# Loading the last 4 KB per partition of wq apart, in transfers of 120 and of 8 partitions

## The chip, the cores and the metric

The kernel runs on one core of a Trainium2 chip. The core has five engines, each with its own instruction queue: PE (TensorE, matrix products), DVE (VectorE), ACT (ScalarE), POOL (GpSimd) and SP (SyncE). Here SP issues nearly all transfers. The transfers themselves run on 16 DMA engines that work beside the five. The metric is the device time of one execution in microseconds (us), as the median over several runs.

## What is computed

One decoding step of a small network for two sequences (B = 2) with one new token each, D = 512. A block of grouped-query attention over a cache of 32,768 positions (32 query heads, 8 key and value heads, head size 128) is joined with a small gated MLP. Cut to what matters:

```python
xn = layernorm(x)
q = (xn @ wq).reshape(B, 1, 32, 128)                   # wq: 512 x 4096
scores = einsum("bhqd,bhkd->bhqk", q, repeat(k_cache, 4)) * 128 ** -0.5
o = einsum("bhqk,bhkd->bhqd", softmax(scores), repeat(v_cache, 4))
s = o.reshape(B, 1, 4096) @ wo                         # wo: 4096 x 512
h2 = gelu(layernorm(x1) @ w3) @ w4                     # the MLP
g = silu(x1 + h2)
return x + s * g
```

With one token per sequence the shifted terms of the mixer are zero, so x1 equals xn, and w1 and w2 aren't needed. All data are bf16. The two caches hold 2 x 8 x 32,768 x 128 x 2 bytes = 134 MB each. They, wq (4 MB), w3, w4 and wo are each read once.

## The kernel before, in words

The work goes over 16 groups, one for each pair of sequence and key head. A group's keys are one transfer of 128 partitions with 64 KB each into `kbuf`, its values one such transfer into `vbuf`. Only the last group is cut into halves. For each group DVE transposes the keys in blocks (line 589), PE forms the scores (line 698), ACT takes the exponentials (line 491), and PE multiplies with the values (line 722). When ACT has seen the end of a group's value products (line 495), SP may issue the next load of values (line 448). When PE has passed the first half of the scores, SP may issue the next load of keys (line 464).

Before the groups there is a prologue. SP issues, in this order and without any wait, wq (line 310, into the third slot of `kbuf`), w3 and w4 (lines 311 and 312, into `vbuf`), the keys of group 0 (line 313), and two small loads of x (line 330). ACT issues one small load of x (line 318). DVE normalises x, and PE transposes it. DVE's copy of the result to `xT` (line 395) is the instruction that waits for wq, with `(d_wq, 16)`. Then PE forms q (line 403), and the MLP's products follow (lines 424 and 439). The load of group 0's values (line 448) waits for the last MLP product, since it overwrites w3 and w4. Four small transfers (line 457) put the gate `g` into the layout of the output.

After the groups comes wo, in six transfers (`wo_parts`, lines 477 and 479). SP issues all of them when ACT has seen the end of the next to last use of their place. PE multiplies each part as it arrives (lines 760 and 768), DVE forms the gated sum (lines 647 and 648), and SP and ACT each store half of the output (line 651).

SP issues in program order. A transfer moves one stretch of memory for each partition row, and the profile counts such stretches as packets. Its semaphore has gone up by 16 when all of it has landed.

`wo_parts` reuses the semaphores of the prologue's loads for its six parts: the first part counts on `d_wq`. `n_wo` holds the value that each part's users wait for.

Of the kernel before, what the change touches and what calls it, by code (L numbers as in the profile page):

```python
# [118 lines left out]
def kernel(  # L119
# [16 lines left out]
    B, Sq, D = A_x.shape  # L136
    _, Hkv, Sk, Dh = A_k_cache.shape
    HD = A_wq.shape[1]
# [4 lines left out]
    DK = D // 128  # L143
# [10 lines left out]
    NQ = 4  # L154
# [3 lines left out]
    OQ = 2  # L158
# [80 lines left out]
    NG = len(groups)  # L239
    wo_parts = [(0, 4, 0, NQ), (4, 5, 0, NQ), (5, 6, 0, NQ), (6, 7, 0, NQ), (7, 8, 1, NQ), (7, 8, 0, 1)]  # L240

    KW = wo_parts[0][1]
    RW = KW * NQ
    FILL = (1, 1)
# [22 lines left out]
    sp = Queue(nc.sync, None)  # L267
# [5 lines left out]
    d_wq, d_w3, d_w4, d_x, d_x4, d_g = (sem(f"d_{n}") for n in ("wq", "w3", "w4", "x", "x4", "g"))  # L273
    d_wo = [d_wq, d_w3, d_w4, d_x, d_x4, d_g]
    assert len(d_wo) == len(wo_parts)
    n_wo = [16, 16, 16, 16, 16 * OQ, 16 * NQ]
    for i in range(len(wo_parts)):
        n_wo[i] += 16

# [7 lines left out]
    kbuf_wq = kbuf[:, 2 * SLOT:3 * SLOT]  # L287
# [19 lines left out]
    with tc.tile_critical(sync_engine=mybir.EngineType.Pool, no_gpsimd_drain=True):  # L307
        nc.scalar.wait_ge(t_shift, n_out).then_inc(t_shift, -n_out)

        sp.op(lambda e: e.dma_start(out=kbuf_wq[:, 0:DK * HD], in_=A_wq.rearrange("(p k) f -> p (k f)", k=DK)), inc=(d_wq, 16))  # L310
        sp.op(lambda e: e.dma_start(out=vbuf[:, 0:W4O], in_=B_w3.rearrange("(p k) f -> p (k f)", k=DK)), inc=(d_w3, 16))
        sp.op(lambda e: e.dma_start(out=vbuf[:, W4O:W4O + FK * D], in_=B_w4.rearrange("(p f) d -> p (f d)", f=FK)), inc=(d_w4, 16))
        sp.op(lambda e: e.dma_start(out=kbuf[:, 0:NPART * SLOT], in_=row_view(A_k_cache, *groups[0])), inc=(t_k[0], 16))
# [9 lines left out]
            out=ident[:, :], in_=ident[:, :], compare_op=ALU.not_equal, fill=1.0, base=0,  # L323
# [14 lines left out]
        e = ve.op(lambda e: e.tensor_copy(out=xf[:, :], in_=x_bf[:, :]), (d_x, 16))  # L338
# [14 lines left out]
        e = e_xn = layernorm(xn, xf, "ln1", e)  # L353
        ve.op(lambda v: v.tensor_copy(out=xs_bf[0:B, :], in_=xn[:, :]), e_xn, e_xs0)
        e = layernorm(ln2, xn, "ln2", e_xn)
        e_xs = ve.op(lambda v: v.tensor_copy(out=xs_bf[32:32 + B, :], in_=ln2[:, :]), e, e_id)  # L356
        with nc.allow_low_precision(reason="one of the terms is one, the others are zero"):
            e = ve.op(lambda v: v.tensor_reduce(
                out=sel0[:, :], in_=ident[:, :].rearrange("p (n w e) -> p w n e", n=NB, e=2), axis=AX.XY, op=ALU.add), e_id)
            e_quad = ve.op(lambda v: v.tensor_reduce(  # L360
                out=quad[:, :], in_=ident[:, :].rearrange("p (j w) -> p j w", j=4), axis=AX.X, op=ALU.add))
        ve.op(lambda v: v.tensor_reduce(
            out=cls[:, :, :], in_=ident[:, :].rearrange("p (n w e) -> p n e w", n=NB, e=2), axis=AX.X, op=ALU.add))
        e_sel = ve.op(lambda v: v.tensor_copy(out=sel[:, :, :], in_=sel0[:, :].unsqueeze(1).broadcast_to([128, 4, 32])), e)
        ve.op(lambda v: v.tensor_reduce(
            out=sel_o[:, :, :],
            in_=ident[:, :].rearrange("p (j a t h) -> p a t h j", j=4, t=VT, h=rep)[:, 0, :, :, :],
            axis=AX.X, op=ALU.add))
        e_selh = ve.op(lambda v: v.tensor_reduce(
            out=sel_h[:, :], in_=ident[:, :].rearrange("p (r h) -> p h r", h=rep), axis=AX.X, op=ALU.add))  # L370
        e_row = ve.op(lambda v: v.tensor_reduce(
            out=row_of[:, :], in_=ident[:, :].rearrange("p (r h) -> p r h", h=rep), axis=AX.X, op=ALU.add))
# [3 lines left out]
            out=comb[:, OJ - 1::OJ], in_=ident[:, :].rearrange("p (n c) -> p c n", n=NQ)[:, 0:B, :], axis=AX.X, op=ALU.add), e_c0)  # L376
        ve.op(lambda v: v.tensor_reduce(
            out=mask[:, :], in_=ident[:, :].rearrange("p (h w) -> p h w", h=rep), axis=AX.X, op=ALU.add))
        ve.op(lambda v: v.tensor_scalar_mul(
            out=same_h[:, :].rearrange("p (r h) -> p r h", h=rep),  # L380
            in0=sel_h[:, :].unsqueeze(1).broadcast_to([128, 32, rep]), scalar1=-inv_sqrt_dh), e_selh)
        e_const = ve.op(lambda v: v.tensor_copy(
            out=sel_w[:, :, :], in_=row_of[:, :].unsqueeze(1).broadcast_to([128, 4, 32])), e_row, e_ones)
# [7 lines left out]
        treg = qrb[:, :].bitcast(BF16)  # L391
        for k in range(DK):
            e = pe.op(lambda t, k=k: t.transpose(  # L393
                out=treg[:, 64 * k:64 * k + 32 + B], in_=xs_bf[:, k::DK], identity=ident[0:32 + B, 0:32 + B]), e_xs)
        e_xT = ve.op(lambda v: v.tensor_copy(
            out=xT[:, :, :].rearrange("p (s k) b -> p s k b", s=2),
            in_=treg[:, 0:64 * DK].rearrange("p (k s c) -> p s k c", k=DK, s=2)[:, :, :, 0:B]), e, (d_wq, 16))
        HH = Hq // NPART
        for i in range(NPART):
            for k in range(DK):  # L400
                for n in range(NQ):
                    last = k == DK - 1 and n == NQ - 1
                    e = pe.op(lambda t, i=i, k=k, n=n: t.matmul(
                        sc[i][32 * n:32 * n + B, :], lhsT=xT[:, k, :],
                        rhs=wq3[:, k, :].rearrange("p (h n y) -> p h n y", n=NQ, y=32)[:, i * HH:(i + 1) * HH, n, :],
                        start=(k == 0), stop=(k == DK - 1), tile_position=(0, 32 * n)),
                        e_xT, e_s00, inc=last)
            e = ve.op(lambda v, i=i: v.transpose(out=qT[:, i * 512:(i + 1) * 512], in_=sc[i][:, :]), e)
        e_q = ve.op(lambda v: v.tensor_mul(
            out=q_sb[:, :, :, :].rearrange("p n e (b h) -> p (n e) b h", b=B),  # L410
            in0=qT[:, :].rearrange("p (h c) -> p c h", c=32)[:, 0:B, :].unsqueeze(1).broadcast_to([128, 2 * NB, B, Hq]),
            in1=cls[:, :, :].rearrange("p n e -> p (n e)").unsqueeze(2).unsqueeze(3).broadcast_to([128, 2 * NB, B, Hq])), e)
        e = pe.op(lambda t: t.matmul(
            qrb[:, 0:NB * 2 * B * Hq], lhsT=sel[:, :, :].rearrange("p j w -> p (j w)"),
            rhs=q_sb[:, :, :, :].rearrange("p n e c -> p (n e c)"), start=True, stop=True), e_q, e_sel)
        e_qr = ve.op(lambda v: v.tensor_copy(
            out=qr[:, :, :, :, :].rearrange("p n e b h -> p (n e b h)"), in_=qrb[:, 0:NB * 2 * B * Hq]), e)
# [3 lines left out]
        for k in range(DK):  # L421
            for n in range(NQ):
                last = k == DK - 1 and n == NQ - 1
                e = pe.op(lambda t, k=k, n=n: t.matmul(
                    pro[32 * n:32 * n + B, 0:FQ], lhsT=xT[:, DK + k, :],
                    rhs=w3v[:, k, n * FQ:(n + 1) * FQ].rearrange("p (y f) -> p f y", y=32),
                    start=(k == 0), stop=(k == DK - 1), tile_position=(0, 32 * n)), (d_w3, 16), inc=last)
        e = ve.op(lambda v: v.transpose(out=h4[:, :], in_=pro[:, 0:FQ]), e)
        e_hf = ve.op(lambda v: v.tensor_copy(
            out=hf[:, :].rearrange("p (f b) -> p f b", b=B), in_=h4[:, :].rearrange("p (f c) -> p f c", c=32)[:, :, 0:B]), e)  # L430
        e = ve.op(lambda v: v.tensor_mul(out=x2[:, :], in0=hf[:, :], in1=hf[:, :]), e_hf)
        e = ve.op(lambda v: v.tensor_scalar(out=x2[:, :], in0=x2[:, :], scalar1=0.044715, scalar2=1.0, op0=ALU.mult, op1=ALU.add), e)
        e = ve.op(lambda v: v.tensor_mul(out=inner[:, :], in0=hf[:, :], in1=x2[:, :]), e)
        e = ac.op(lambda v: v.activation(out=th[:, :], in_=inner[:, :], func=ACT.Tanh, scale=GELU_C), e)
        e = ve.op(lambda v: v.tensor_scalar(out=th[:, :], in0=th[:, :], scalar1=0.5, scalar2=0.5, op0=ALU.mult, op1=ALU.add), e)
        e = ve.op(lambda v: v.tensor_mul(out=h_bf[:, :], in0=hf[:, :], in1=th[:, :]), e, (d_w4, 16))
# [6 lines left out]
        e = ac.op(lambda v: v.activation(out=sig[:, :], in_=t_f[:, :], func=ACT.Sigmoid), e_tf)  # L443
# [17 lines left out]
        for m in range(1, NG):  # L461
            base = m % 2
            if m < NG - 1:
                sp.op(lambda e, m=m, base=base: e.dma_start(
                    out=kbuf[:, base * SLOT:(base + NPART) * SLOT], in_=row_view(A_k_cache, *groups[m])),
                    (pe.sem, pe_0 + m), e_q, inc=(t_k[0], 16))
            else:
                for i, h in enumerate(order(m)):
                    sp.op(lambda e, m=m, h=h, base=base: e.dma_start(
                        out=kbuf[:, (base + h) * SLOT:(base + h + 1) * SLOT],  # L470
                        in_=row_view(A_k_cache, *groups[m])[:, h * SLOT:(h + 1) * SLOT]),
# [14 lines left out]
        with nc.Fori(0, NG // 2, engines=[ACTE]):  # L486
            for par in range(2):
                take(nc.scalar, t_shift)
                for h in range(NPART):
                    i = order(par).index(h)  # L490
                    nc.scalar.activation(  # L491
                        out=ep[i][:, :], in_=sc[i][:, :], func=ACT.Exp, scale=inv_sqrt_dh, bias=shift[:, :],
# [84 lines left out]
        with nc.body("dve_groups", valid_engines=[DVE]):  # L577
            c = Counts()
            for par in range(2):
                nc.vector.wait_ge(*c(t_z))  # L580
                for i, h in enumerate(order(par)):
                    u = par + h
                    kt = kbuf[:, u * SLOT:(u + 1) * SLOT].bitcast(I32)
                    for r in range(NR):
                        n = i * NR + r
                        events = ([c(t_k[i], 16)] if r == 0 else []) + ([used(par, n - T_BUFS)] if n >= T_BUFS else [])
                        for e in events[:-1]:
                            nc.vector.wait_ge(*e)
                        ins = nc.vector.transpose(  # L589
                            out=Ts[n % T_BUFS][:, :].rearrange("p (b t k) -> p t b k", b=NB, t=RT),  # L590
                            in_=kt[:, r * W:(r + 1) * W].rearrange("p (t b k) -> p t b k", b=NB, t=RT))
# [10 lines left out]
                for h in range(NPART):  # L602
                    e = c(t_e)
# [33 lines left out]
        c = Counts()  # L637
# [174 lines left out]
```

## Time and profile before

| what | value |
|---|---|
| median of 3 runs | 655.92 us (655.91 to 655.99) |
| profiled execution, span from first to last instruction | 654.1 us |
| PE busy in the span | 417.4 us (64%) |
| DVE busy | 379.4 us (58%) |
| ACT busy, POOL busy | 39.7 us, 10.3 us |
| bytes moved | 280.54 MB, mean 429 GB/s |
| share of 16 DMA engines on SP's queue (q1) | 99.2% |

The profiled execution gives its span and no total of its own. The span and the median differ by 1.8 us, which lies before the first and behind the last instruction or in the profiling.

The profile has a page with busy times, slices, queues, the chain that ended last and groups of instructions. Its trace can be asked for a window of time. A view of DMA for a window gives two rows of 40 equal slices (the busy share of the 16 engines in tenths, where 9 means 90% or more, and GB/s). Below stand the packets that started in the window and, per queue, packets, MB, and the time of these packets as a share of 16 engines over the window. So share x 16 x window / packets is the mean time of a packet, and a share can go over 100% where packets run out of the window. A row of the timeline gives start, duration, engine, line, operation, operands and count. In brackets stands how long the engine was idle before and who ended that. "SPq" is an issue by SP, not the transfer.

### The profile page before, as it was taken

How to read it: one execution, taken by the hardware profiler on the slowest of the kernel's cores; microseconds unless marked ns; L12 is line 12 of the kernel's file. 1: busy time of each engine (PE TensorE's matmuls, PEld its weight loads, DVE VectorE, ACT ScalarE, POOL GpSimd, SP SyncE). 2: the span in 40 equal slices, each digit the busy share in tenths (PEclk: the TensorE clock that was granted, in tenths of full speed). 3: DMA queues.
4: the chain of work that ended last, by engine and by line, in shares of the span. 5: the costliest groups of instructions: out<-in, count | busy, mean ns of one | idle time of the engine just before them, and what ended most of it. 6: DMA issues, size and time to landing. Idle time of an engine off the chain costs nothing. (4 is left out here: it accounts for less than half of the span.)

```text
span 654.1 us, 6304 instructions
## 1 busy us (share of the span) xinstructions
PE 417.4 (64%) x2476; PEld 159.3 (24%) x2476; DVE 379.4 (58%) x541; ACT 39.7 (6%) x90; POOL 10.3 (2%) x44
## 2 busy tenths in 40 slices
PE   1437386574858747485774838667484865748876
PEld 0013132221313212131321313222131322213223
DVE  5348193673919457291854729276481936738772
ACT  1200101000010100001000010100001010000101
POOL 1000000000000000000000000000000000000000
PEclk9859889697997969899796989969698896979999
DMA  8999999999999999998999999999999899999997
GB/s 367 435 449 449 442 393 449 445 449 401 437 445 449 433 405 449 445 449 389 449 445 449 417 421 445 449 445 393 449 445 449 389 449 445 449 425 411 437 429 292
DMA packets 6246, 280.54 MB, mean 429 GB/s; under 512 B 730, under 2 KB 868, under 8 KB 1380
## 3 DMA queue, kind: packets, MB, share of 16 engines
q1 hardware_dynamic: 6232, 280.50, 99.2%
q8 instruction: 2, 0.03, 0.0%
q10 hardware_dynamic: 12, 0.00, 0.0%
HBM read 280.50 MB, written 0.00 MB: 429 GB/s over the span
## 5 line engine op out<-in xcount | busy, mean ns | idle before, releaser
L589 DVE STREAM_TRANSPOSE T<-kbuf 128x1024 int32<-128x1024 int32 x256 | 294.8, 1211 | 180.1 <-DMA kbuf<-in_A_k_cache_dram 173.2
L698 PE MATMUL sc<-T,z 128*128 128x512 bf16 x1024 | 273.1, 420 | 179.5 <-PEq L482 179.2
L698 PEld LDWEIGHTS sc<-T,z 128*128 128x128 bf16 x1024 | 98.9, 104 | 346.6 <-issue 260.2
L722 PE MATMUL o<-vbuf,pt 128*16 128x512 bf16 x1024 | 70.4, 379 | 17.7 <-PEq L482 17.7
L491 ACT ACTIVATE ep<-sc,shift 128x512 bf16<-128x512 f32 x32 | 21.7, 683 | 502.7 <-ACTq L482 502.7
L722 PEld LDWEIGHTS o<-vbuf,pt 128*16 128x16 bf16 x1024 | 27.3, 88 | 64.9 <-issue 42.8
L568 DVE TENSOR_REDUCE mx<-sc 128x1 f32<-128x512 f32 x32 | 21.5, 672 | 30.1 <-PE sc L698 30.1
L673 PE MATMUL pro<-ob,comb 128*2 128x512 f32 x66 | 33.7, 592 | 0.0
L608 DVE STREAM_TRANSPOSE pt<-ep 128x512 bf16<-128x512 bf16 x32 | 22.6, 708 | 15.0 <-ACT ep L491 15.0
L710 PE MATMUL S<-mxr,same_h 128*128 128x448 f32 x32 | 15.8, 576 | 18.4 <-PEq L482 18.4
L660 PEld LDWEIGHTS oT<-sel_o,ob 128*128 128x128 f32 x136 | 17.7, 191 | 3.4 <-issue 0.7
L729 PE MATMUL S<-sm,ones_f 128*128 128x448 f32 x32 | 16.3, 592 | 0.0
L660 PE MATMUL oT<-sel_o,ob 128*128 128x4 f32 x136 | 16.2, 242 | 0.0
L600 DVE TENSOR_REDUCE shift<-S 128x1 f32<-128x64 f32 x16 | 3.6, 225 | 18.8 <-PE S L710 18.8
L496 ACT COPY ob<-o 128x512 f32<-128x512 f32 x16 | 9.4, 587 | 78.6 <-ACTq L482 78.6
L513 POOL COPY oX<-oXs 128x4 bf16 (+1 forms) x16 | 3.0, 188 | 518.7 <-POOLq L482 518.7
L710 PEld LDWEIGHTS S<-mxr,same_h 128*128 128x128 f32 x32 | 4.8, 188 | 26.1 <-issue 26.1
L572 DVE TENSOR_SCALAR mxr<-row_of,mx 128x32 f32<-128x32 f32 x32 | 7.7, 241 | 1.1
L673 PEld LDWEIGHTS pro<-ob,comb 128*2 128x2 f32 x66 | 4.2, 83 | 14.0 <-issue 10.4
L393 PE MATMUL qrb<-ident,xs_bf 34*128 34x34 bf16 x4 | 0.3, 198 | 11.1 <-DVE xs_bf L356 11.1
L729 PEld LDWEIGHTS S<-sm,ones_f 128*128 128x128 f32 x32 | 4.8, 188 | 6.9 <-issue 6.9
L506 POOL TENSOR_TENSOR z<-qr,quad 128x64 bf16<-128x64 bf16 x16 | 4.7, 294 | 103.2 <-POOLq L482 87.7
(100 smaller groups left out, 78.5 us busy)
## 6 DMA issues: line engine op xcount, KB each, us to landing
kbuf<-in_A_k_cache_dram SPq DMA_DIRECT2D x2, 4096.0 KB, 22.4
vbuf<-in_A_v_cache_dram SPq DMA_DIRECT2D x2, 4096.0 KB, 21.7
kbuf<-in_A_wq_dram SPq DMA_DIRECT2D x1, 4096.0 KB, 12.4
vbuf<-in_B_w_dram SPq DMA_DIRECT2D x2, 1792.0 KB, 18.0
kbuf<-in_A_wo_dram SPq DMA_DIRECT2D x1, 2048.0 KB, 30.8
kbuf<-in_A_wo_dram SPq DMA_DIRECT2D x3, 512.0 KB, 31.9
kbuf<-in_A_wo_dram SPq DMA_DIRECT2D x1, 384.0 KB
kbuf<-in_A_k_cache_dram SPq DMA_DIRECT2D x15, 27.5
```

The costliest lines, as they stand in the source:

```text
L491: nc.scalar.activation(out=ep[i][:, :], in_=sc[i][:, :], func=ACT.Exp, scale=inv_sqrt_dh, bias=shift[:, :], accum_out=rs[:, i:i + 1]).then ...
L496: nc.scalar.copy(out=ob[:, :], in_=o[:, :]).then_inc(t_ob, 1)
L568: ins = nc.vector.tensor_reduce(out=mx[:, i:i + 1], in_=sc[i][:, :], axis=AX.X, op=ALU.max)
L572: ins = nc.vector.tensor_scalar_mul(out=mxr[:, i, :], in0=row_of[:, :], scalar1=mx[:, i:i + 1]).wait_op(*c.at(t_d), "sem-ge")
L589: ins = nc.vector.transpose(out=Ts[n % T_BUFS][:, :].rearrange("p (b t k) -> p t b k", b=NB, t=RT), in_=kt[:, r * W:(r + 1) * W].rearrange ...
L608: ins = nc.vector.transpose(out=pt[h][:, :, :].rearrange("p r (t h) -> p t r h", h=rep), in_=ep[order(par).index(h)][:, :].rearrange("p (t ...
L660: ins = nc.tensor.matmul(oT[:, :], lhsT=ob[:, t * Dh:(t + 1) * Dh], rhs=sel_o[:, t, :], start=(t == 0), stop=(t == VT - 1))
L673: nc.tensor.matmul(pro[0:B, :], lhsT=comb[:, 0:B], rhs=ob[:, :], start=True, stop=True)
L698: ins = nc.tensor.matmul(sc[i][:, :], lhsT=z[:, nb, w, zc:zc + 128], rhs=Tb[:, nb, :, w], start=(r == 0 and nb == 0 and w == 0), stop=(r = ...
L710: nc.tensor.matmul(S[:, NPART * rep:NPART * (rep + SREP * 32)].rearrange("p (s c) -> p s c", s=SREP), lhsT=same_h[:, :], rhs=mxr[:, :, :]. ...
L722: ins = nc.tensor.matmul(o[32 * j:32 * j + VT * rep, :], lhsT=pt[h][:, r, a * VT * rep:(a + 1) * VT * rep], rhs=vt[:, u * VT:(u + 1) * VT, ...
L729: nc.tensor.matmul(S[:, 0:SSUM * NPART * rep].rearrange("p (s c) -> p s c", s=SSUM), lhsT=ones_f[:, :], rhs=sm[:, :, :].rearrange("p i h - ...
```

## The change

The 128 partition rows of wq are 32 KB long each. The kernel before loads them in one transfer. The changed kernel loads the first 28 KB of all 128 rows in one transfer, then the last 4 KB of rows 0 to 119 in a second and of rows 120 to 127 in a third. All three go into the same places as before and count on the same semaphore. So DVE's copy (line 395 before) waits for 48 in place of 16, and the first part of wo waits for 64 in place of 32.

```diff
+    wq_parts = [(0, 128, 0, DK * HD - 2048), (0, 120, DK * HD - 2048, DK * HD), (120, 128, DK * HD - 2048, DK * HD)]
...
-    n_wo = [16, 16, 16, 16, 16 * OQ, 16 * NQ]
+    n_wo = [16 * len(wq_parts), 16, 16, 16, 16 * OQ, 16 * NQ]
...
-        sp.op(lambda e: e.dma_start(out=kbuf_wq[:, 0:DK * HD], in_=A_wq.rearrange("(p k) f -> p (k f)", k=DK)), inc=(d_wq, 16))
+        wq_rows = A_wq.rearrange("(p k) f -> p (k f)", k=DK)
+        for p0, p1, c0, c1 in wq_parts:
+            sp.op(lambda e, p=slice(p0, p1), c=slice(c0, c1): e.dma_start(out=kbuf_wq[p, c], in_=wq_rows[p, c]), inc=(d_wq, 16))
...
-            in_=treg[:, 0:64 * DK].rearrange("p (k s c) -> p s k c", k=DK, s=2)[:, :, :, 0:B]), e, (d_wq, 16))
+            in_=treg[:, 0:64 * DK].rearrange("p (k s c) -> p s k c", k=DK, s=2)[:, :, :, 0:B]), e, (d_wq, 16 * len(wq_parts)))
```

On SP the change adds two issues of transfers. PE, DVE, ACT and POOL have the same instructions in the same order as before; line numbers behind the edit go up by 4.

## The prediction

> **What bounds the kernel now.** I read the page's DMA rows first, then the chain that ended last, then DMA windows at the end. On the page and in a long window inside the groups, SP's queue:
>
> ```profile
> span 654.1 us, 6304 instructions
> q1 hardware_dynamic: 6232, 280.50, 99.2%
> q8 instruction: 2, 0.03, 0.0%
> ```
>
> ```profile
> q1 hardware_dynamic: 4002, 233.90, 100.0%
> ```
>
> The second fence is the window from 60 to 600 us: 16 engines are busy for 540 us without a gap. PE at 64% and DVE at 58% wait for it. So the time is set by bytes per DMA engine, and the engine that finishes last sets the end. The chain that ended last, in order of time (start, duration):
>
> ```profile
> 617.12 33.53 DMA kbuf<-in_A_wo_dram
> 650.64 0.04 issue
> 650.69 0.64 PE pro L768 x16
> 651.33 0.02 issue
> 651.35 0.29 DVE sg L647
> ```
>
> From 617 us on it is wo, then 3.4 us of fixed tail (654.1 - 650.7). The question is whether all 16 engines end together. The window from 648 to 652 us in slices of 0.1 us, and then 649.7 to 650.7 us alone:
>
> ```profile
> DMA  9899999999997627100000000000000000000000
> GB/s 420 348 379 440 471 399 440 379 359 359 420 328 256 215 92 215 41 31 31 31 0 31 31 21 20 20 21 0 0 0 0 0 0 0 0 0 0 0 0 0
> ```
>
> ```profile
> DMA packets 15, 0.02 MB, mean 24 GB/s; under 512 B 2, under 2 KB 10, under 8 KB 15
> q1 hardware_dynamic: 15, 0.02, 6.2%
> ```
>
> They don't. In the second window 6.2% x 16 x 1.0 us = 0.99 us of packets run in 1.0 us: one engine works without pause and 15 are done. In the slices the last packet of another engine starts between 649.6 and 649.7 (41 GB/s there is 4.1 KB, a 3 KB piece of the late engine and 1 KB of another), and the late one's last between 650.6 and 650.7. So one engine is late by 1.0 us, give or take 0.1.
>
> Where does the delay come from? Windows 71.5 to 72.6, then 72.69 to 72.71 and, for an ordinary 64 KB packet, 72.1 to 72.2:
>
> ```profile
> q1 hardware_dynamic: 14, 0.92, 192.4%
> q8 instruction: 1, 0.02, 5.2%
> ```
>
> ```profile
> q1 hardware_dynamic: 1, 0.07, 914.1%
> ```
>
> ```profile
> q1 hardware_dynamic: 1, 0.07, 151.1%
> ```
>
> An instruction fetch of 16 KB holds one engine for 5.2% x 16 x 1.1 = 0.92 us. The packet that starts behind it lasts 914.1% x 16 x 0.02 = 2.93 us, where the ordinary one takes 151.1% x 16 x 0.1 = 2.42 us. That engine loses 0.92 + 0.51 = 1.43 us, once. Since no engine pauses afterwards, the loss stays to the end. One that had been 0.4 us ahead of the last would end 1.0 late: the sizes fit, though the rows don't number engines. The page counts two fetches; the second falls at the end, where 15 engines have little left.
>
> **The change part by part.** Packet times first: windows 6 to 11 us (32 KB rows of wq), 14 to 16.5 (14 KB) and 646 to 646.6 (4 KB rows of wo).
>
> ```profile
> q1 hardware_dynamic: 64, 2.10, 97.0%
> ```
>
> ```profile
> q1 hardware_dynamic: 78, 1.12, 104.3%
> ```
>
> ```profile
> q1 hardware_dynamic: 63, 0.26, 104.3%
> ```
>
> 97.0% x 16 x 5 / 64 = 1.213 us for 32 KB; 104.3% x 16 x 2.5 / 78 = 0.535 us for 14 KB; 104.3% x 16 x 0.6 / 63 = 0.159 us for 4 KB. On the line through the first two, 28 KB takes 0.535 + 14/18 x 0.678 = 1.062 us.
>
> First, the spread. The first 16 packets start together (window 1.9 to 2.6), so 128 rows lie 8 to an engine; the load of x with 2 rows puts 2 packets on ACT's queue (3.9 to 4.1):
>
> ```profile
> q1 hardware_dynamic: 16, 0.52, 273.7%
> ```
>
> ```profile
> q10 hardware_dynamic: 2, 0.00, 2.8%
> ```
>
> Rows are thus the unit that is dealt out. 128 = 16 x 8, 120 = 15 x 8, and 8 rows go one to an engine. I take 15 engines with 8 rows and 8 engines with 1 row; no row here shows a transfer of 120, so other ways of dealing stand among the rivals. [...]
>
> Per engine, wq costs 8 x 1.213 = 9.70 us before. After, with the long part (8 x 1.062 = 8.50) everywhere:
> - one engine gets nothing more: 8.50, that is 1.20 less.
> - seven get 8 x 0.159 = 1.27 more: 9.77, that is 0.07 more.
> - eight get a further 0.159: 9.93, that is 0.23 more.
>
> All 16 together get 1.20 - 7 x 0.07 - 8 x 0.23 = 1.1 us more work: the change makes nothing cheaper, it only moves load off one engine.
>
> Second, the two issues on SP. The prologue's rows:
>
> ```profile
> 0.90 0.40 SPq L310 DMA_DIRECT2D kbuf<-in_A_wq_dram  x1
> 1.36 0.41 SPq L311 DMA_DIRECT2D vbuf<-in_B_w_dram  x1
> 2.86 0.93 SPq L330 DMA_DIRECT2D x_bf<-in_A_x_dram  x2
> 13.29 0.17 DVE L395 COPY xT<-qrb 128x16 bf16<-128x16 bf16 x1 [0.18 <-DMA kbuf<-in_A_wq_dram]
> 27.45 0.36 SPq L448 DMA_DIRECT2D vbuf<-in_A_v_cache_dram  x1
> ```
>
> Two more at 0.46 us from start to start (1.36 - 0.90) move w3, w4, the keys and the x loads back by 0.92 us. Past them are queued only these four kinds, and each engine has 8.5 us of the first part to do from 1.9 us on, so none runs dry: nothing. If that cover were gone it would be 0.92 us.
>
> Third, the wait. DVE's copy would run with wq's last landing, up to 0.23 us later than 13.29, and with it q and the MLP; the issue at 27.45 goes back by as much. What hides it is the group 0 keys, until their landing:
>
> ```profile
> 41.14 1.25 DVE L589 STREAM_TRANSPOSE T<-kbuf 128x1024 int32<-128x1024 int32 x1 [10.51 <-DMA kbuf<-in_A_k_cache_dram]
> ```
>
> The keys keep the engines busy for 41.14 - 27.45 = 13.7 us beyond that issue, and DVE idles 10.51 us before them. Without that cover it would cost 0.23 us. Neither edit reaches the path.
>
> Sum, if the relieved engine is the late one: it comes 1.20 us earlier, which is past the next engine, 1.0 us ahead of it. The end is then set by that next one with its 0.07 or 0.23 us: a gain of 0.77 to 0.93, with the 0.1 of the lag 0.67 to 1.03. I take the middle, 0.87. PE could take over behind it:
>
> ```profile
> 649.07 0.81 PE L750 MATMUL pro<-T,comb 128*4 128x128 f32 x8
> 649.74 0.61 PE L768 MATMUL pro<-kbuf,oXz 128*4 128x128 bf16 x16
> 650.69 0.62 PE L768 MATMUL pro<-kbuf,oXz 128*4 128x128 bf16 x16 [0.33 <-DMA kbuf<-in_A_wo_dram]
> ```
>
> PE idles 0.33 us before the last group, and the two steps ahead also follow parts of wo that the late engine brings. With all parts up to 1 us earlier they move along, so PE takes nothing back. The sum is made within the 654.1 us of the profiled execution and laid on the median: 655.92 - 0.87 = 655.05 us.
>
> **The rivals.**
> - The late engine is one of the seven. It carries 0.07 us more, the end moves by that: 655.99. For it speaks that nothing numbers the engines and a fetch could sit anywhere.
> - It is one of the eight, on the other side: 0.23 us more on the engine that sets the end, 656.15. This decides as soon as the late one is dealt one of rows 120 to 127; nothing hides it, since 15 engines are done for 1.0 us before it.
> - The rows are dealt otherwise. With 120 rows over eight engines, 15 to each, these get 7 x 0.159 + 0.23 = 1.34 us more: 655.92 + 1.34 = 657.26 if the late one is among them, 656.2 if only the next one is (1.34 - 1.0). All on one engine would be 120 x 0.159 - 1.2 = 17.9 us: 673.8. For it: no transfer of 120 rows in this trace. Against it: the 2 rows above went out as 2 packets, and 8 rows per engine is the way of the 128.
> - Each transfer drains the engines before the next. The only price near is the load of x by ACT, whose first user starts at 5.56 after an issue at 1.06, 4.5 us with all its queueing:
>
> ```profile
> 1.06 0.55 ACTq L318 DMA_DIRECT2D x_bf<-in_A_x_dram  x1
> 5.56 0.41 DVE L338 CAST shared<-x_bf 2x512 f32<-2x512 bf16 x1 [2.30 <-DMA x_bf<-in_A_x_dram]
> ```
>
> Two drains cost between 0 and 9 us, up to 664.9, and decide against the gain from 0.45 us each. The 540 us at 100.0% speak against it: 233.90 MB in loads of 8.4 MB are some 28 transfers, one behind another. [...]
>
> **How the numbers follow.** Relieved engine is the late one: 0.62. One of the seven: 0.17. One of the eight: 0.12. Dealt otherwise: 0.06. Drains: 0.03. The first is a judgement: by count it would be 1 in 16. I go far above that because the loss comes from a fetch, a fixed duty of single engines, and such a duty is likelier put at an end of the row of engines than in its midst. Rows dealt from the front leave the last engine out, and a fetch kept away from the front would sit there; the trace doesn't settle it. [...]
>
> The predicted time is 655.05, with its own range of 654.85 to 655.25. The range goes on to the seven and the eight: 654.8 to 656.25, which leaves out 0.09. About 0.2% (1.31 us) is what a measurement of this kernel can tell from no change. The first three cases all lie inside that, as does part of the fourth. Faster by more needs a larger lag in the runs than in the profiled execution, 0.03; slower by more is the drains and the worst of the dealing, 0.05; within it 0.92.
>
> **What would show it.** Right: the lone engine at the end is gone, so that the last packets of wo stop within 0.3 us of one another, DMA lands about 0.9 us earlier before the last products (line 772 after), and a few packets of 4 KB appear near 10 to 12 us on 15 engines. The fetch near 72 us stays. Wrong: the 1.0 us with one engine stays at the end, or grows to 1.2; or gaps in the DMA slices before 13 us; or the copy to `xT` starts later than 13.6 us.

## The result and the profile after

The changed kernel takes 657.33 us (657.11 to 657.57, 13 runs), beside 655.86 us for the kernel before (655.62 to 656.43, 13 runs): 1.0021 times as long [1.0013, 1.0029], 1.47 us more. The forecast was 0.87 us less. The profiled execution tells the same: its span went from 654.1 to 655.5 us.

The page of the kernel after:

```profile
span 655.5 us, 6274 instructions
q1 hardware_dynamic: 6383, 280.50, 99.2%
q8 instruction: 2, 0.03, 0.0%
```

Bytes and busy share are as before, so the transfers still set the time. The queue was as busy, but longer. Where it lost the time shows in what had been started by 11 us and by 17 us, first in the kernel before:

```profile
DMA packets 116, 3.67 MB, mean 334 GB/s; under 512 B 2, under 2 KB 4, under 8 KB 4
...
DMA packets 306, 6.25 MB, mean 367 GB/s; under 512 B 33, under 2 KB 35, under 8 KB 35
```

The same windows, 0 to 11 and 0 to 17 us, in the kernel after:

```profile
DMA packets 132, 3.67 MB, mean 334 GB/s; under 512 B 2, under 2 KB 4, under 8 KB 4
...
DMA packets 398, 5.62 MB, mean 330 GB/s; under 512 B 41, under 2 KB 43, under 8 KB 171
```

By 11 us both have started 3.67 MB. By 17 us the kernel after is 6.25 - 5.62 = 0.63 MB behind. At 0.43 MB per us (the 429 GB/s of the whole run) that is 1.5 us, the whole loss. So it is made between 11 and 17 us, where the 4 KB pieces and the first rows of w3 run. The engines aren't idle there. This is the window from 11 to 15 us of the kernel after (DMA slices, then the queue):

```profile
DMA  0175979979999979799999999966650490993966
...
q1 hardware_dynamic: 205, 1.07, 98.5%
```

Both rows count the packets that began in the window, so the first slice is empty while 28 KB rows from before it still run. The 98.5% says that the engines are busy; they are slow. The window from 12.12 to 13.01 us holds, but for 4 short ones, pieces of 4 KB alone:

```profile
DMA packets 54, 0.20 MB, mean 230 GB/s; under 512 B 4, under 2 KB 4, under 8 KB 54
...
q1 hardware_dynamic: 54, 0.20, 95.3%
```

95.3% x 16 x 0.89 us / 50 = 0.271 us for a piece, against the 0.159 us that the prediction took from wo. Over all 128 pieces of 4 KB the trace's mean is 0.246 us; eight at 0.087 us more are 0.7 us on each engine. About as much again falls on what runs beside and behind them. The window from 13.6 to 15.5 us holds 4 short packets and 39 rows of 14 KB:

```profile
q1 hardware_dynamic: 43, 0.56, 77.6%
```

77.6% x 16 x 1.9 us / 39 = 0.605 us for a row, against 0.535 us before. Over the 256 rows of w3 and w4 the mean is 0.577 us, so the 16 rows of an engine lose another 0.7 us.

At the other end nothing has changed. The window from 649 to 653 us (slices of 0.1 us), then 651.1 to 652.0 alone:

```profile
DMA  7997999969999988742710000000000000000000
GB/s 317 410 543 318 369 369 492 440 246 410 379 379 430 359 307 307 266 164 92 225 41 31 31 0 31 31 21 20 31 10 0 0 0 0 0 0 0 0 0 0
```

```profile
q1 hardware_dynamic: 14, 0.02, 6.0%
```

6.0% x 16 x 0.9 us = 0.86 us of packets in 0.9 us: again one engine works alone, from about 651.1 to 652.0. All engines end some 1.3 us later, and the late one is as late as it was. The timeline around the change and at the end:

```profile
0.90 1.25 SPq L314 DMA_DIRECT2D kbuf<-in_A_wq_dram  x3
2.19 0.36 SPq L315 DMA_DIRECT2D vbuf<-in_B_w_dram  x1
...
14.89 0.17 DVE L399 COPY xT<-qrb 128x16 bf16<-128x16 bf16 x1 [1.88 <-DMA kbuf<-in_A_wq_dram]
...
31.14 0.35 SPq L452 DMA_DIRECT2D vbuf<-in_A_v_cache_dram  x1
...
652.03 0.61 PE L772 MATMUL pro<-kbuf,oXz 128*4 128x128 bf16 x16 [0.37 <-DMA kbuf<-in_A_wo_dram]
```

SP issues three transfers in 1.25 us. The copy to `xT` comes 14.89 - 13.29 = 1.6 us later, the values of group 0 are issued 3.7 us later (31.14 against 27.45), and the last products start 652.03 - 650.69 = 1.34 us later.

### The profile page after: what moved, and what is told of

Read it like the earlier page. It is cut to its first block, busy times and chain, and to the rows that moved or that the text cites. A ratio compares the mean times of both kernels' runs of the same rounds, so it can differ in the third digit from the quotient of the medians.

```text
span 655.5 us, 6274 instructions
## 1 busy us (share of the span) xinstructions
PE 415.2 (63%) x2444; PEld 160.8 (25%) x2476; DVE 379.8 (58%) x541; ACT 39.7 (6%) x90; POOL 10.3 (2%) x44
## 5 line engine op out<-in xcount | busy, mean ns | idle before, releaser
L702 PE MATMUL sc<-T,z 128*128 128x512 bf16 x992 | 268.7, 422 | 181.4 <-PEq L486 180.0
L443 PE MATMUL sc<-vbuf,h_bf 128*2 128x512 bf16 x14 | 4.9, 525 | 2.4 <-DVE h_bf L440 2.4
```

The source lines that it names most:

```text
L702: ins = nc.tensor.matmul(sc[i][:, :], lhsT=z[:, nb, w, zc:zc + 128], rhs=Tb[:, nb, :, w], start=(r == 0 and nb == 0 and w == 0), stop=(r = ...
```

## The experiments

Unless a diff is said to be against the kernel before, it is against the changed one. Times are medians, each beside the kernel before on the same chip. Three suspects stood at first: that short pieces or a further transfer cost time in themselves (theory S in the expectations), that unevenly dealt rows do (U), and that engines hinder one another when their pieces go to the same group of partitions (P).

**One further transfer, all 128 rows.**

```diff
-    wq_parts = [..., (0, 120, DK * HD - 2048, DK * HD), (120, 128, DK * HD - 2048, DK * HD)]
+    wq_parts = [..., (0, 128, DK * HD - 2048, DK * HD)]
```

> The last 4 KB of wq apart, but in one transfer of all 128 rows. Theory P (rows dealt other than 8 of 128 make two engines write into the same stretch of partitions, and their packets take up to twice the time): no such dealing here, so packets of 4 KB at 0.16 us and 655.9 us, at most 0.1 more. Theory S (short pieces, or one more transfer at this place, cost): 4 KB packets stay at 0.25 us and about half to all of the 1.4 us comes back, 656.6 to 657.3. Theory U (uneven work per engine costs): 655.9.

Measured: 656.13 beside 655.95 us, ratio 1.0003 [0.9993, 1.0012]. Its window from 11.2 to 12.3 us:

```profile
DMA packets 125, 0.45 MB, mean 410 GB/s; under 512 B 15, under 2 KB 15, under 8 KB 125
...
q1 hardware_dynamic: 125, 0.45, 100.1%
```

100.1% x 16 x 1.1 / 110 = 0.160 us for a piece, the 0.159 us of wo. Neither the short pieces nor one more transfer costs anything that this measurement can tell.

**Two halves of 64 rows.**

```diff
-    wq_parts = [..., (0, 120, DK * HD - 2048, DK * HD), (120, 128, DK * HD - 2048, DK * HD)]
+    wq_parts = [..., (0, 64, DK * HD - 2048, DK * HD), (64, 128, DK * HD - 2048, DK * HD)]
```

> The last 4 KB of wq in transfers of rows 0 to 63 and 64 to 127: every engine has 8 pieces, none is relieved. Theory P: two engines meet in each stretch all the time, 4 KB packets near 0.31 us, 8 x 0.15 = 1.2 us on every engine, 657.1 us. Theory U: the work is even, so 655.9 us and 0.16 us a packet. Theory S: as long as with 120 and 8, 657.3. [...]

Measured: 657.07 beside 655.95 us, ratio 1.0018 [1.0009, 1.0028]. Window 12.0 to 12.4 us:

```profile
DMA packets 37, 0.11 MB, mean 277 GB/s; under 512 B 10, under 2 KB 10, under 8 KB 37
...
q1 hardware_dynamic: 37, 0.11, 116.3%
```

116.3% x 16 x 0.4 / 27 = 0.276 us for a piece. Here 64 rows divide evenly by 16, and yet most of the loss is back, as theory P had it. So uneven dealing isn't needed: here two transfers over half of the partitions each were enough, with 0.276 us for a piece against 0.160 in the transfer over all 128.

**The same cut, twice the size.**

```diff
-    wq_parts = [(0, 128, 0, DK * HD - 2048), (0, 120, DK * HD - 2048, DK * HD), ...]
+    wq_parts = [(0, 128, 0, DK * HD - 4096), (0, 120, DK * HD - 4096, DK * HD), ...]
```

> Transfers of 120 and of 8 rows again, but with the last 8 KB in place of 4. Theory P: twice the bytes at the low rate, so about twice the loss, 655.9 + 2.8 = 658.7 us, and the relieved engine's semaphore steps are early by about 1.9 us instead of 0.9. Theory S (a cost per transfer): 657.3 as with 4 KB. If the relieved engine were the late one the loss would not double, since the time would follow the others' next largest load only.

Measured: 659.32 beside 655.95 us, ratio 1.0052 [1.0035, 1.0069]. Window 11 to 14 us:

```profile
DMA packets 84, 0.70 MB, mean 232 GB/s; under 512 B 2, under 2 KB 2, under 8 KB 2
...
q1 hardware_dynamic: 84, 0.70, 107.4%
```

The rate of 232 GB/s is that of the 4 KB pieces (230), for twice the bytes. The loss of 3.4 us is a little more than twice 1.47: it goes with the bytes and not with the number of transfers.

**The last 4 KB in 16 transfers of 8 rows, spread or neighbouring.** In the first, a transfer takes every fourth row of a block of 32; in the second, 8 neighbouring rows.

```diff
+    wq_parts = [(0, 128, 1, 0, DK * HD - 2048)] + [(32 * h + i, 32 * h + 32, 4, DK * HD - 2048, DK * HD) for h in range(4) for i in range(4)]
...
+    wq_parts = [(0, 128, 0, DK * HD - 2048)] + [(p, p + 8, DK * HD - 2048, DK * HD) for p in range(0, 128, 8)]
```

> The last 4 KB of wq in 16 transfers of 8 rows, every fourth row of a block of 32, so that eight engines have 16 pieces each and eight have none. Theory P (two engines that write into the same group of partitions share its rate; the groups are those that the transfer of 128 rows gives to one engine each): every fourth row lies in another group, so the pieces of rows 0 to 63 take 0.16 us; those of rows 64 to 127 meet the other eight engines, which have gone on to w3 there, and take up to 0.31. The eight engines end 1.3 to 2.5 us later, on the next latest engine 0.3 to 1.5 us more than before: 656.2 to 657.4 us. Theory N (fewer than 16 engines at 8 rows each is slow as such): 0.25 to 0.31 us from the first piece on.

> The same 16 transfers of 8 rows, but 8 rows next to each other. Same engines, same bytes per engine, same count. Theory P: 8 neighbouring rows lie in two groups, four engines to each, so a piece takes about 4 x 0.16 = 0.64 us and the 16 pieces 10 us in place of 1.3: about 8 us more than before, 664. Theory N: as with every fourth row, 656.2 to 657.4.

Measured beside 656.02 us: spread 657.79, ratio 1.0026 [1.0017, 1.0036]; neighbouring 658.49, ratio 1.0039 [1.0025, 1.0054]. The 17 issues on SP, and the queue from 11 to 15 us, spread:

```profile
0.89 11.28 SPq L314 DMA_DIRECT2D kbuf<-in_A_wq_dram  x17
```

```profile
q1 hardware_dynamic: 299, 0.91, 70.8%
```

and neighbouring:

```profile
0.89 6.25 SPq L314 DMA_DIRECT2D kbuf<-in_A_wq_dram  x17
```

```profile
q1 hardware_dynamic: 302, 1.12, 104.8%
```

A spread issue takes 11.28 / 17 = 0.66 us, and the engines run dry (70.8%), so that pair didn't separate the two as meant. The neighbouring form was busy throughout and lost 2.5 us, far less than the 8 us that the strong form of the theory wanted. The spread form, at 657.79 us, also lies outside the 656.2 to 657.4 us that both theories gave it.

**Crossed: which side matters.** The last 16 KB of wq are loaded for 64 rows only, in 8 transfers of 8; the other half is left out and zeroed by DVE. Rows read and partitions written are each spread or neighbouring, in four kernels. In the diff, which is shortened, WRITTEN and READ stand for one of the two lists below.

```diff
+    cut = DK * HD - 8192
+    wq_parts = [(slice(0, 128), slice(0, 128), slice(0, cut))] + [(o, i, slice(cut, DK * HD)) for o, i in zip(WRITTEN, READ)]
...
+    spread = [slice(32 * h + i, 32 * h + 29 + i, 4) for h in range(2) for i in range(4)]
+    neighbouring = [slice(p, p + 8) for p in range(0, 64, 8)]
```

> A cost by itself, with work left out: the last 16 KB of wq in 8 transfers of 8 rows, for rows 0 to 63 only (the other half is set to zero by DVE), so that eight engines have 8 pieces of 16 KB each. Destination and source rows are every fourth row of a block of 32. At the full rate a piece takes 0.61 us. Theory P (engines that write into one group of four partitions share its rate): eight groups, 0.61 us. Theory R (the reading side: rows of the source that lie close): 0.61 us too. The time itself isn't compared; eight engines have less to load.

> As before it, but each transfer reads 8 neighbouring rows and writes them to every fourth partition (the data land in other rows than they should). P: 0.61 us a piece. R: slower, towards what neighbouring rows give on both sides.

> Each transfer reads every fourth row and writes 8 neighbouring partitions (the data land in other rows than they should; the other half of wq's last 16 KB is left out as before). P: four engines to a group, up to 4 x 0.61 = 2.4 us a piece and 20 us for eight, less where engines drift apart to other groups. R: 0.61 us.

> 8 neighbouring rows on both sides, the rest as in the three before. P: as with neighbouring partitions alone, up to 2.4 us a piece. R: as slow as neighbouring source rows alone. If neither side alone is slow but both are, it is neither.

Measured in one execution each: to spread partitions 655.38 (spread rows) and 655.0 us (neighbouring rows); to neighbouring partitions 665.24 and 665.68. Packets from 9 to 17 us, spread to spread, then neighbouring rows to spread partitions:

```profile
DMA packets 270, 3.14 MB, mean 392 GB/s; under 512 B 57, under 2 KB 57, under 8 KB 57
```

```profile
DMA packets 269, 3.12 MB, mean 390 GB/s; under 512 B 57, under 2 KB 57, under 8 KB 57
```

Spread rows to neighbouring partitions, then neighbouring to neighbouring:

```profile
DMA packets 107, 1.12 MB, mean 140 GB/s; under 512 B 34, under 2 KB 34, under 8 KB 34
```

```profile
DMA packets 110, 1.15 MB, mean 143 GB/s; under 512 B 35, under 2 KB 35, under 8 KB 35
```

In these transfers of 8 rows the partitions written decide, 390 to 392 against 140 to 143 GB/s; which rows are read makes no such difference. That engines which write to neighbouring partitions at the same time hold one another up is the reading of these rows; by what means isn't shown. The expectation for that, up to 2.4 us a piece and 20 us for eight, was an upper bound; the two kernels lost some 9 to 10 us against the 656.02 us before.

**Which engine is late.** Against the kernel before, 15 small loads (the marks) of 1, 2, ... 15 rows of 512 B, ahead of the keys of group 5. If transfers of fewer rows leave out the last engines, each engine gets its own number of marks.

```diff
+            if m == 5:
+                for i in range(1, 16):
+                    sp.op(lambda e, i=i: e.dma_start(out=marks[i * (i - 1) // 2:i * (i + 1) // 2, :], in_=A_wo[0:i, 0:256]), inc=(d_marks, 16))
```

> The kernel before, with 15 small loads of 1, 2, ... 15 rows of 512 bytes each queued between the values of group 4 and the keys of group 5, into a place of their own that nothing reads. If rows are dealt from the first engine on, engine e (counted from 0) gets 15 - e of these packets, which tells the number of the late engine from how many pass after the other 15 engines have gone on, near 216 us. My prediction's first case: the late one is the last, none. The trace after the change, where one engine lands early and another late: between 1 and 15 of them. The time goes up by 0.4 us at most, less the further back the late engine stands.

Measured: 709.51 us, one execution. First the window from 212.2 to 213.5 us, where one engine starts its last 64 KB packet of the load ahead of the marks behind all others (near 213.10; with 2.42 us it ends near 215.51). Then the packets from 213.5 to 215.515 us, and the window from 215.515 to 215.634 (slices of 3 ns):

```profile
q1 hardware_dynamic: 1, 0.07, 11.6%
...
DMA packets 252, 0.97 MB, mean 484 GB/s; under 512 B 127, under 2 KB 238, under 8 KB 238
...
DMA  5000000010500000001050000000705000010100
GB/s 172 0 0 0 0 0 0 0 1 0 172 0 0 0 0 0 0 0 1 0 172 0 0 0 0 0 0 0 173 0 172 0 0 0 0 1 0 1 0 0
DMA packets 10, 0.00 MB, mean 22 GB/s; under 512 B 5, under 2 KB 10, under 8 KB 10
```

238 - 127 = 111 marks have started before, most of them by 214.7. The 127 packets under 512 B are 111 + 16, one to a mark and 16 of the load ahead; so I take it that each row of the marks' loads has an engine of its own. Then four follow at even steps of ten slices (0, 10, 20, 30), by their spacing from one engine; the one in slice 28 falls out of step and I take it for another's. The last four of the 120 start between 215.9 and 216.5, behind the late engine's next 64 KB packet (215.634). Four marks belong to the twelfth engine in the order of dealing, number 11 from 0. A transfer of 120 rows over 15 engines includes it: the late engine is one of the seven.

That the 120 rows go over 15 engines and the 8 rows over eight fits the packets under 512 B, in the whole execution before, then after:

```profile
DMA packets 6246, 280.54 MB, mean 429 GB/s; under 512 B 730, under 2 KB 868, under 8 KB 1380
...
DMA packets 6397, 280.54 MB, mean 428 GB/s; under 512 B 753, under 2 KB 891, under 8 KB 1531
```

The two further transfers bring 753 - 730 = 23 of them, as one to an engine would: 15 + 8.

The traces without marks show in another way that it isn't the relieved one. Packets of 64 KB follow one another on an engine every 2.41 us, so an engine that has fallen out of step shows up alone in the gap between two rounds of the others. In the kernel before, the gap from 69.8 to 71.4 us, ahead of the fetch that the prediction found, is empty; the gap from 598.65 to 600.55 us holds one packet:

```profile
DMA packets 0, 0.00 MB, mean 0 GB/s; under 512 B 0, under 2 KB 0, under 8 KB 0
```

```profile
q1 hardware_dynamic: 1, 0.07, 8.0%
```

Followed from packet to packet in the trace, that one is the engine that did the fetch near 72 us. It began the fetch 0.38 us before the last engine began its packet of that round, as the prediction had supposed. So the fetch is where the lag begins. In the kernel after, the gap from 73.6 to 75.4 us, ahead of the fetch, holds one packet; the gap from 76.0 to 77.8, behind it, holds two. The third row is the window from 600.1 to 601.85 us:

```profile
q1 hardware_dynamic: 1, 0.07, 8.4%
```

```profile
q1 hardware_dynamic: 2, 0.13, 18.6%
```

```profile
GB/s 0 0 0 0 0 0 0 0 0 0 0 0 0 0 0 0 0 0 0 1498 0 749 0 0 0 0 0 0 0 0 0 0 0 0 0 0 0 0 0 0
```

The packet alone ahead of the fetch is the relieved engine's: followed back to the prologue it has eight pieces of 28 KB and none of 4 KB. It stays ahead, and near 601.05 us it starts a 32 KB row (749 GB/s x 0.044 us) before any of the fourteen in step. The engine that did the fetch starts its last 64 KB packet near 600.95 us, which ends near 603.36, 0.9 us after the last of the fourteen. The relieved engine and the late one are two.

The run had a second effect that nobody expected. Ahead of the marks (100 to 190 us), and behind them (230 to 290 us):

```profile
q1 hardware_dynamic: 660, 39.06, 100.1%
...
q1 hardware_dynamic: 405, 23.40, 101.0%
```

A packet takes, over all sizes, 100.1% x 16 x 90 / 660 = 2.18 us ahead and 101.0% x 16 x 60 / 405 = 2.39 us behind; without the short ones (64 and 48), 2.42 and 2.72 us. It stays at that to the end.

Two more runs gave marks of even number: 8 loads of 16 rows, and 15 loads of 8 rows.

```diff
+                for i in range(8):
+                    sp.op(lambda e, i=i: e.dma_start(out=marks[16 * i:16 * i + 16, :], in_=A_wo[0:16, 0:256]), inc=(d_marks, 16))
...
+                for i in range(15):
+                    sp.op(lambda e, i=i: e.dma_start(out=marks[8 * i:8 * i + 8, :], in_=A_wo[0:8, 0:256]), inc=(d_marks, 16))
```

> The small marks of 512 bytes again, at the same place, but in 8 transfers of 16 rows: every engine gets 8. With the graded marks every 64 KB packet after them took 2.71 us in place of 2.42, to the end, and the time was 709.5 us. Theory G (the engines' being spread over the time of a packet costs rate for as long as it lasts): here the engines stay level, packets stay at 2.42 and the time is 655.9 plus at most 1 us. Theory M (small packets or marks as such leave the slow rate behind): 2.71 us and about 709 again.

> 15 transfers of 8 rows: eight engines get 15 marks each, 0.45 us at 0.03 us a mark, the other eight none. G: two level groups 0.45 us apart, less than the 1.0 us of the late engine, which does no harm before: packets stay at 2.42; the first eight are still ahead of the late engine at the end if it is number 11, so 655.9 to 656.3 us. M: 2.71 us and about 709. If the late engine is one of the first eight: 656.4.

Measured: 656.98 and 657.74 us beside 655.78, one execution each. Both have this row from 230 to 590 us; it is quoted from the run with 16 rows. Behind it stand, of the run with 8 rows, the windows from 651 to 652, from 215.5 to 217.25 and from 215.3 to 215.5 us:

```profile
q1 hardware_dynamic: 2688, 156.24, 100.1%
```

```profile
q1 hardware_dynamic: 103, 0.18, 47.2%
```

```profile
DMA packets 2, 0.07 MB, mean 37 GB/s; under 512 B 1, under 2 KB 1, under 8 KB 1
```

```profile
q1 hardware_dynamic: 58, 0.54, 1028.6%
```

In the first, 100.1% x 16 x 360 / (2688 - 304 short ones) = 2.42 us: no slow rate. So marks alone don't bring it, nor eight engines that run behind the others; why the graded ones did stays open. In the second, 47.2% x 16 = 7.6 engines are at work in the last microsecond: the eight that were marked end last, and the lone engine is hidden ahead of them. The third shows where that engine stands. It goes from its last 64 KB packet of the load before (start near 213.56 us) to the next (near 215.98), 2.42 us later, and the window between holds that packet and one of a few bytes, but no mark. So it isn't one of the first eight, which agrees with number 11 without proving it. The fourth shows why this run took 657.74 us where 655.9 to 656.3 was expected: eight 64 KB packets behind the marks and 50 short ones take 1028.6% x 16 x 0.2 = 32.9 us, so some 4 us for each long one, once. Why they are so slow stays open.

**Load on the late engine.** Against the kernel before, an unused load of 16 KB pieces into free space, for 11 rows and for 12. If the rows go one to an engine from the first on, only the second reaches number 11.

```diff
+        sp.op(lambda e: e.dma_start(out=vbuf[0:41:4, W4O + FK * D:W4O + FK * D + 8192], in_=...[0:11, 0:8192]), inc=(d_w4, 16))
```

> The kernel before with one more load ahead of group 0's keys: 11 rows of 16 KB into every fourth partition of a free place, which nothing reads. If rows go to the first engines in order, engines 0 to 10 get one piece of 0.61 us each, up to 1.2 where two meet, and the late engine, number 11 by the small marks, none: the lag of 1.0 us covers it and the time stays at 655.9, at most 0.3 more. If the late engine is below 11: 0.6 to 1.2 us more.

> The same with 12 rows. Engine 11 now gets a piece too, 0.61 us, up to 1.2 where two engines meet (its row lies in one group with the fourth): if it is the late one, 656.5 to 657.1. If the late engine stands further back than 11, 655.9 to 656.2 as with 11 rows.

Measured beside 656.08 us: 656.84, ratio 1.0011 [1.0001, 1.002], and 659.08, ratio 1.0047 [1.0027, 1.0067]. The first lost 0.76 us where at most 0.3 was expected. The second lies from 656.96 to 661.18, a scatter that no theory had. The direction is that of number 11, the size isn't explained; on its own this pair settles nothing.

**What relief of the late engine at the end is worth.** Against the kernel before, the 3 KB part of wo goes to the first eight engines, for rows 0 to 63 alone; the rest of that part is left out. Then, complete, the last 1 KB part in 16 transfers of 8 spread rows.

```diff
+            if i == 4:
+                for p0 in [32 * h + q for h in range(2) for q in range(4)]:
+                    sp.op(... out=wo3[p0:p0 + 29:4, a:c, cols] ...)
...
+            if i == 5:
+                for p0 in [32 * h + q for h in range(4) for q in range(4)]:
+                    sp.op(... out=wo3[p0:p0 + 29:4, a:c, cols] ...)
```

> The kernel before, with work left out: of the 3 KB part of wo (the last but one) only rows 0 to 63 are loaded, in 8 transfers of every fourth row, so that eight engines have their 8 pieces as before and the other eight none; the products read what lies there. The packets of the kernel with small marks put the late engine at number 11, among the eight relieved. Then it ends 8 x 0.12 = 0.94 us earlier and the time falls by 0.9, to 655.0. If the late engine is one of the first eight, or if the lone engine at the end isn't what sets the time: 655.9.

> A version meant to beat both: the kernel before, with the last part of wo (1 KB of each row) in 16 transfers of every fourth row, all on the first eight engines, which at that time wait for the late one. The late engine ends 8 x 0.043 = 0.34 us earlier, the eight end 0.34 later plus 16 completions and still before it: 655.6, a gain of 0.3 us in the profile's last landing. If the late engine is among the first eight: 0.4 us more, 656.3.

Measured beside 656.02 us: 655.63, ratio 0.9995 [0.9985, 1.0004], and 658.01, ratio 1.003 [1.0018, 1.0042]. DMA from 648 to 652 us and PE's last group, with half of the part left out:

```profile
GB/s 379 410 287 390 389 359 430 154 287 205 164 215 225 154 72 31 31 10 0 0 0 0 0 0 0 0 0 0 0 0 0 0 0 0 0 0 0 0 0 0
```

```profile
649.79 1.06 PE L772 MATMUL pro<-kbuf,oXz 128*4 128x128 bf16 x32
```

The data end by 649.8 and the lone engine is gone, so it is one of the eight that had no piece of this part. But PE now runs 32 products without a wait. Its end came from 650.69 + 0.62 = 651.31 to 649.79 + 1.06 = 650.85: 0.46 us, and then PE is the bound. The expected 0.9 us is missed by that; the medians differ by 0.39 us, with no change inside the interval. With 16 small transfers, the issues and the last wait:

```profile
617.95 24.48 SPq L481 DMA_DIRECT2D kbuf<-in_A_wo_dram  x16
...
653.58 0.28 PE L772 MATMUL pro<-kbuf,oXz 128*4 128x128 bf16 x4 [1.67 <-DMA kbuf<-in_A_wo_dram]
```

An issue takes 24.48 / 16 = 1.5 us here, but all are out by 642.4 us. The last data start before 651.0 us in that trace, and PE's wait for them ends only at 653.58, later by more than the relief could bring. Why the landing shows so late stays open.

The last attempt was meant to deal the last part to engines ahead of number 11, in two transfers, of 88 and 40 rows: of 1 KB as before, then cut at 2 KB.

```diff
+            rows = (slice(0, 88), slice(88, 128)) if i == 5 else (slice(0, 128),)
...
-    wo_parts = [..., (7, 8, 1, NQ), (7, 8, 0, 1)]
+    wo_parts = [..., (7, 8, 2, NQ), (7, 8, 0, 2)]
```

> A version meant to beat both: the kernel before, with the last part of wo (1 KB a row) in transfers of 88 rows (11 engines) and of 40 rows (10 engines), so that the late engine, number 11 by the marks, gets none of it. It ends 8 x 0.043 = 0.34 us earlier; ten engines get 12 pieces in place of 8, 0.17 us more at the full rate, 0.7 at half of it, both still about level with the late one: a gain of 0.2 to 0.35 us in the profile's span, 655.7 us. If the late engine is below 10: 0.2 to 0.7 us more.

> The same with the last 2 KB a row. The late engine ends 8 x 0.083 = 0.66 us earlier. Ten engines get 12 pieces in place of 8, 0.33 us more at the full rate and 1.3 at half: a gain of 0.6 us at the full rate, a loss of 0.3 at half.

Measured beside 656.02 us: 656.14, ratio 1.0001 [0.9992, 1.001], and 656.68, ratio 1.001 [1.0001, 1.0019]. PE's last groups, in this order:

```profile
651.39 0.61 PE L770 MATMUL pro<-kbuf,oXz 128*4 128x128 bf16 x16 [0.44 <-DMA kbuf<-in_A_wo_dram]
```

```profile
650.43 1.23 PE L770 MATMUL pro<-kbuf,oXz 128*4 128x128 bf16 x32 [0.57 <-DMA kbuf<-in_A_wo_dram]
```

In both runs 735 packets are under 512 B, where the kernel before has 730: 5 more, as with 11 and 10 engines in place of 16. Which engines they were isn't shown. In the first PE still waits for a landing; in the second it waits for the part before and runs back to back from there. Neither brought the expected gain (0.2 to 0.35 us for the first), and the second lost 0.66 us. No complete version beat the kernel before.

## Why the prediction was wrong

- **The case chosen.** The step that failed first is the judgement that the late engine is the one left out (0.62). The lone engine at the end is still there after the change, 0.86 of 0.9 us; in the same trace the relieved engine is still 0.85 us ahead of all others at 601 us, and the marks put the late one at number 11. The run with 8-row marks and the one with half a part of wo left out exclude the first eight engines too. The argument that a fetch is a fixed duty and sits at an end of the row of engines had no row behind it: the trace before shows a fetch that held one engine for 0.92 us, and doesn't show on which engines fetches fall. By the prediction's own list that leaves the rival with the seven, 655.99 us.
- **The term that was mis-sized.** That rival missed too, by 1.3 us, as did the one with the eight. "Seven get 8 x 0.159 = 1.27 more" took the piece of 4 KB from a transfer over 128 rows. In the transfer over 120 rows a piece took 0.271 us (0.246 on average over all 128 pieces), and the rows of w3 behind it were slowed as well, 0.605 against 0.535 us, so every engine lost some 1.4 us, the late one with them. The crossed runs point to the side written: 140 to 143 GB/s into neighbouring partitions, 390 to 392 into spread ones. How the 120 rows are dealt inside the transfer wasn't seen. That the loss comes from which partitions are written at the same time, and not from something else about 120 rows, rests on the halves (0.276 us) and the run with 8 KB.
- **The groups of partitions in the expectations.** They count four neighbouring partitions to a group, and up to four engines that share one group's rate. That was the author's assumption, and no run shows such groups. Shown are 0.276 against 0.160 us for a piece in the halves, and in the crossed runs 140 against 390 GB/s over a window that also holds other packets. With 4 KB pieces the estimate was far too high: 16 pieces of four times 0.159 us on each of eight engines would have cost some 9 us (16 x 0.64 - 1.27), and 2.5 were lost.
- **The rival that was named and given little.** Drains between transfers (0.03) isn't it: the queue is at 98.5% in the stretch of the loss, and a further transfer of 128 rows cost nothing measurable (ratio 1.0003). Nor is dealing over eight engines: these would fill 50% of 16 at most, and the pieces of 4 KB fill 95.3%. That this rival's 657.26 us lies beside the measured 657.33 is a coincidence.
- **What held.** The two issues on SP are covered: three go out in 1.25 us, and the engines have work till 11 us. So is the wait on wq, though it moved by 1.6 us and not by 0.23: the values of group 0 went out 3.7 us later and the keys still ended after. The dealing over 15 engines and over eight fits the 23 more packets under 512 B. The time is set by the bytes per engine to the end, the tail behind is unchanged, and a fetch is still there, now in the window from 75.2 to 76.4 us:

```profile
q8 instruction: 1, 0.02, 5.0%
```

- **"PE takes nothing back"** would have failed too. With the lone engine gone at the end, PE gave 0.46 us and was then the bound itself. Those runs relieved the end alone; relief in the prologue, as the prediction had it, wasn't tried on the right engine.
- **The sum.** Two slips in it are too small to matter: the middle of 0.77 and 0.93 us is 0.85 and not 0.87, and the terms of the 1.1 us of added work stand with the wrong signs. The work added was far more: 1.4 us on each of 16 engines.
- **The chances.** Slower by over 0.2% had 0.05, and the median came out 0.22% slower. But for the drains no case held a slowdown of all engines, since each took the piece's time as fixed by its size.

That the fetch makes the engine late rests on the order in two traces: the engines are in step ahead of it but for the relieved one, and the engine that did it is alone behind them from there to the end. No run took the fetch away.

## What to carry to other kernels

In these runs the time of a packet went with its size (0.159 us for 4 KB, 1.213 us for 32 KB) and with the partitions of its transfer (4 KB took 0.160 us in one over all 128, 0.271 in one over 120, 0.276 in halves); take a price only from a transfer with the same spread of partitions, and let the range hold a factor of two where there is none. Here a transfer over all 128 partitions cost nothing measurable when it was cut along the free axis (ratio 1.0003), and a cut along the partitions made its pieces take some 1.7 times as long while it ran. Before work is moved off a late engine, find out which one it is, and what would be the bound once it is relieved.

## What the runs showed of the hardware that was not expected

- In the crossed runs only the side written to mattered: 390 to 392 GB/s into spread partitions and 140 to 143 into neighbouring ones, whatever the rows read.
- An issue on SP isn't a fixed price: 0.42 us (1.25 / 3) for three contiguous blocks, 0.66 us for 8 rows at every fourth partition, 1.5 us for such a transfer at the end of the kernel. What the last ones waited for isn't shown.
- One instruction fetch of 16 KB near 72 us, 0.92 us long, still showed as a lag of 1.0 us at 650 us: with the queue at 100.0% from 60 to 600 us the engine never caught up.
- Fifteen small loads of graded size left the later 64 KB packets 12% slower, 2.72 against 2.42 us, for more than 400 us; fifteen of 8 rows each, and eight of 16, didn't. The cause is open.
